# A written-out order of operations replaced by another: warming products first, keys loaded in halves, block means of v transposed once per batch

## The chip, the core and the metric

The kernel runs on one NeuronCore of one Trainium2 chip. The metric is the device time of one execution in microseconds (us). Three runs of the kernel before gave 411.3, 411.57 and 408.1 us.

## The reference

Four batches, 768 positions, 8 heads of 64. Attention of each query over its near keys (less than 16 positions away) and over 24 block summaries, one for each 32 positions: the maximum of the keys, the mean of the values. Its output, 512 wide, goes through a gated layer with a product over positions.

```python
k_sum = k.reshape(B, H, nb, 32, D).max(axis=3)
v_sum = v.reshape(B, H, nb, 32, D).mean(axis=3)
scores_l = scale * q @ k.T            # kept where |i - j| < 16
scores_s = scale * q @ k_sum.T + log(32)
a = softmax(concat(scores_l, scores_s));  x = a @ concat(v, v_sum)
h = maximum(x @ w_in, 0);  u, v = h[..., :512], h[..., 512:]
v_n = (v - mean(v)) / sqrt(var(v) + 1e-6)
v_s = w_spatial @ v_n + b_spatial[:, None]     # over positions
out = (u * v_s) @ w_out
```

## The kernel before

**Attention.** A group is one batch `b`, one third `c` of its queries (256 positions) and one half `g` of its heads: 24 groups. For each there is a block of scores (`s{b}_{c}_{g}`, 32 instructions, line 431), a softmax (`m...`: masked minimum on VectorE at line 444, exponential on ScalarE at line 448, normalisation at line 459 or 461 on ScalarE, VectorE or GpSimd), a transpose of the probabilities (`t...`, lines 480 and 488) and the product with the values (`x...`, line 504). The keys come from HBM as one tile for each batch and pair of heads (`key_load`, `k{b}_{pr}`, 544 KB); `key_prep` (tag `p{b}_{pr}`) takes maxima on VectorE (line 359) and ScalarE copies them behind the keys of each segment (line 369). Of batch 0 the block means of v come from a product (`vsums`, tag `vs`, line 384); of batches 1 to 3 from `vmean` (tag `vm`): one load of `vT`, one sum on VectorE (line 403) and one transpose on TensorE (line 407) for each of the four pairs of heads.

**The gated layer.** Every product is three products of split numbers (a high and a low part, both fp32r, `mm3`, line 538): `pv` (the half of `w_in` for v), `pu` (the half for u), `sp` (over positions), `po` (output). The weights come in 64-bit words and are converted by `split64`, a chain of seven to nine operations on ScalarE, VectorE and GpSimd; for the four pieces `wi1_*` of the v half three products on TensorE (lines 298 to 300) make the low part, which ScalarE then copies out. The first product of `pv0_0` or `pv0_1` waits for all four pieces `wi1_*` and for `x0_0_0` and `x0_0_1` (line 539: the first step carries the needs of all).

**The order.** `Plan` collects operations; each can run on the engines it names. `ORDER` lists them all: two characters of base 64 are the number of an operation, a digit is its engine (0 PE, 1 VectorE, 2 ScalarE, 3 GpSimd, 4 the DMA queue of SyncE). `Plan.order` places them in this order and works out a start for each, with its own constants for engines, lags and transfers. Each engine, and the one queue SP that issues nearly all loads and stores, then executes its operations strictly in the listed order. The starts are used for one more thing: as long as the warming product `warm` (128 x 120, two instructions) has a last use ahead, lines 731 to 733 put one more of them in front of a TensorE operation for each 330 ns of planned idle time. In the table of before the first warming product stands eleventh on TensorE, after `s0_1_0`; its last use follows `t0_1_1`.

The last output tile (`last`, lines 632 to 636) is evicted from PSUM in two halves of 64 partitions, one by ScalarE with a store from ScalarE's queue, one by VectorE with a store from SP.

Of the kernel before, what the change touches and what calls it, by code (L numbers as in the profile page):

```python
# [9 lines left out]
F32 = mybir.dt.float32  # L10
# [27 lines left out]
ONES = QB + (NT - 1) * (P // SBLK)  # L38
# [25 lines left out]
class Plan:  # L64
# [7 lines left out]
    TURN_ROUND, TURN_OVER = 187, 143  # L72
# [4 lines left out]
    def add(self, engs, fn, pri, w=(), r=(), port=False, xfer=0, mode="d", lat=0, tag=None):  # L77
# [7 lines left out]
        op.ready = op.start = op.end = 0  # L85
        after = set()
# [20 lines left out]
    def order(self):  # L107

        free = dict(SP=730, POOL=5500)
# [39 lines left out]
        while pool:  # L149
            op, e = listed[len(made)] if listed else choose()  # L150
            at = max([a.end if a.eng == e else a.done for a in op.after], default=0)
# [29 lines left out]
            for u in op.users:  # L181
                u.need -= 1
                u.ready = max(u.ready, op.end if e == "PE" and "PE" in u.engs else done + (SLACK if "PE" in u.engs and not listed else 0))
                if not u.need:
                    pool.append(u)
# [6 lines left out]
def tile_local_summary_attention_gmlp(ctx: ExitStack, tc: tile.TileContext, qT, kext, vext, vnat, vT, w_in, w_sp, b_rep, w_out, out):  # L192
# [49 lines left out]
    def dma(out_, in_, kb, pri, w=(), r=(), issue=400, rate=RATE, tag=None):  # L242
# [104 lines left out]
    def key_load(b, pr, pri):  # L347
        kt = k_sb[b, pr] = Buf(att, [P, KC], F32, "k", f"k{b}_{pr}")
        dma(lambda: kt.t, kext[b, pr], 544, pri, w=[kt], tag=f"k{b}_{pr}")

    def key_prep(b, pr, pri):
        kt = k_sb[b, pr]
        gm = Buf(small, [P, 52], F32, "gm", f"gm{b}_{pr}")
        plan.tag = f"p{b}_{pr}"

        def emit(e):
            t, g = kt.t, gm.t
            kv = t[:, :NSEG * SEG].rearrange("p (s c) -> p s c", c=SEG)
# [461 lines left out]
def psa_ns(n):  # L820
    return 58 + n * 0.828
# [60 lines left out]
```

## Time and profile before

| | us |
|---|---|
| median of three runs | 411.3 |
| the profiled execution | 409.42 |
| its span, first to last instruction | 407.6 |
| PE (TensorE matmul) busy in it | 388.2 |
| DVE (VectorE) busy | 277.4 |
| ACT (ScalarE) busy | 196.8 |
| POOL (GpSimd) busy | 62.6 |
| mean granted TensorE clock (1 is 2.4 GHz) | 0.989 |

Times in rows are microseconds from the start of the span, durations in microseconds or, where a mean of one instruction is given, in nanoseconds. A line number is that of the kernel before.

### The profile page before, as it was taken

To read this page: it belongs to the slowest core of one execution; us is meant where nothing else is said; L and a number is where in the kernel's file an instruction comes from. 1 tells how busy PE (TensorE), PEld (TensorE's weight loads), DVE (VectorE), ACT (ScalarE), POOL (GpSimd) and SP (SyncE) were. 2 spreads that over 40 slices of the span, in tenths; PEclk is the share of its full clock that TensorE was granted. 3 is DMA by queue.
4 is the path that set the end of the run, shared out by engine and by line. 5 is a ranking of instruction groups with operands and counts; after the bars stand their busy time and mean duration, and the time that the engine had idled before them with its cause. 6 is when DMAs were issued, how large, how long until landed. Compare 5 with 4: busy or idle time off the path is not lost.

```text
span 407.6 us, 9242 instructions
## 1 busy us (share of the span) xinstructions
PE 388.2 (95%) x3496; PEld 323.4 (79%) x3496; DVE 277.4 (68%) x964; ACT 196.8 (48%) x645; POOL 62.6 (15%) x91
## 2 busy tenths in 40 slices
PE   2798989999999999999999999999999999999995
PEld 0367868888988888898888888898888888888884
DVE  3989999999956777875675478776786324744421
ACT  2889987886655276642053356635245212200111
POOL 3036556302220002020000030010000000200000
PEclk9969999999999999999999999999999999999998
DMA  8989899530204754301046242302222001000012
GB/s 282 406 240 285 254 303 317 143 112 2 90 28 166 225 193 143 104 7 61 0 117 197 73 158 66 92 2 67 66 67 90 27 2 53 2 0 0 27 51 77
DMA packets 18684, 46.86 MB, mean 115 GB/s; under 512 B 2512, under 2 KB 3280, under 8 KB 18512
## 3 DMA queue, kind: packets, MB, share of 16 engines
q1 hardware_dynamic: 18560, 46.15, 36.1%
q8 instruction: 27, 0.44, 0.4%
q10 hardware_dynamic: 80, 0.13, 0.1%
q14 instruction: 17, 0.14, 0.1%
HBM read 39.98 MB, written 6.29 MB: 114 GB/s over the span
## 4 chain that ended last, share of the span: by engine, by line
PE 87%; DMA 5%; DVE 3%; ACT 2%; SPq 1%; issue 1%; POOL 1%; DVEq 0%
PE sp L538 24%; PE po L538 15%; PE pu L538 15%; PE pv L538 15%; PE s L431 6%; PE x L504 6%; DMA k<-in_kext_dram 3%; PE t L488 3%; PE t L480 1%; DMA wi<-in_w_in_dram 1%; SPq L243 1%; ACT p L448 1%; DVE gm L359 1%; PE wwi L298 0%; POOL p L461 0%
## 5 line engine op out<-in xcount | busy, mean ns | idle before, releaser
L448 ACT ACTIVATE p<-p,sums 128x120 f32<-128x120 f32 x192 | 73.7, 387 | 6.3 <-DVE sums L444 6.1
L538 PE MATMUL sp<-wsp_h,vnh 128*128 128x512 f32 (+1 forms) x192 | 65.2, 339 | 0.0
L538 PE MATMUL sp<-wsp_l,vnh 128*128 128x512 f32 (+1 forms) x192 | 64.6, 337 | 0.0
L538 PE MATMUL sp<-wsp_h,vnl 128*128 128x512 f32 (+1 forms) x192 | 64.6, 336 | 0.0
L444 DVE CUSTOM_DVE_ANT_0 p<-s,mask 128x120 f32<-128x120 f32 x192 | 42.2, 276 | 12.7 <-PE s L431 12.7
L538 PE MATMUL po<-wo_h,gt 128*128 128x512 f32 x128 | 46.2, 395 | 0.0
L538 PE MATMUL pu<-xh,win_h 128*128 128x512 f32 (+1 forms) x128 | 43.8, 342 | 0.0
L606 DVE TENSOR_TENSOR g<-sp,brep 128x512 f32<-128x512 f32 (+1 forms) x32 | 17.3, 555 | 38.5 <-PE sp L538 38.2
L538 PE MATMUL pu<-xl,win_h 128*128 128x512 f32 (+1 forms) x128 | 43.1, 337 | 0.0
L538 PE MATMUL pu<-xh,win_l 128*128 128x512 f32 (+1 forms) x128 | 43.1, 337 | 0.0
L538 PEld LDWEIGHTS sp<-wsp_h,vnh 128*128 128x128 f32 x192 | 36.4, 190 | 4.5
L538 PEld LDWEIGHTS sp<-wsp_l,vnh 128*128 128x128 f32 x192 | 36.4, 190 | 4.1
L538 PEld LDWEIGHTS sp<-wsp_h,vnl 128*128 128x128 f32 x192 | 36.4, 190 | 3.8
L538 PE MATMUL pv<-win_h,xh 128*128 128x512 f32 x96 | 38.5, 401 | 0.8 <-DVE g L606 0.8
L572 POOL TENSOR_TENSOR mv<-mv,mhalf 128x1 f32<-128x1 f32 x24 | 14.5, 605 | 154.7 <-DVE mv L571 142.7
L538 PE MATMUL po<-wo_l,gt 128*128 128x512 f32 x96 | 37.6, 391 | 0.0
L538 PE MATMUL pv<-win_l,xh 128*128 128x512 f32 x96 | 37.6, 391 | 0.0
L538 PE MATMUL pv<-win_h,xl 128*128 128x512 f32 x96 | 37.4, 390 | 0.0
L448 ACT ACTIVATION_READ_ACCUMULATOR p<-p,sums 128x1 f32 x192 | 36.5, 190 | 0.0
L249 ACT COPY pt<-t 120x512 f32<-120x512 f32 x31 | 17.9, 584 | 28.5 <-PE t L488 25.2
L253 ACT ACTIVATE u<-pu 128x256 f32<-128x256 f32 (+1 forms) x27 | 13.0, 485 | 37.3 <-PE pu L538 37.2
L569 DVE BATCH_NORM_STATS2 mv<-vf 128x6 f32<-128x512 f32 x24 | 16.5, 687 | 19.0 <-ACT vf L253 19.0
(128 smaller groups left out, 766.1 us busy)
## 6 DMA issues: line engine op xcount, KB each, us to landing
k<-in_kext_dram SPq DMA_DIRECT2D x16, 544.0 KB, 7.2
qd<-in_qT_dram SPq DMA_DIRECT2D x24, 256.0 KB, 4.4
ve<-in_vext_dram SPq DMA_DIRECT2D x24, 256.0 KB, 3.9
out_dram<-ob SPq DMA_DIRECT2D x23, 256.0 KB, 2.0
vt<-in_vT_dram SPq DMA_DIRECT2D x12, 384.0 KB, 4.8
wi<-in_w_in_dram SPq DMA_DIRECT2D x6, 512.0 KB, 7.2
ve<-in_vext_dram SPq DMA_DIRECT2D x24, 128.0 KB, 3.6
wo<-in_w_out_dram SPq DMA_DIRECT2D x8, 256.0 KB, 5.4
```

Source lines behind the costliest of these rows:

```text
L243: add(("SP", issue), lambda e: nc.sync.dma_start(out=out_() if callable(out_) else out_, in_=in_() if callable(in_) else in_), pri, w, r, ...
L249: (nc.scalar.copy if e == "ACT" else nc.vector.tensor_copy)(out=out_, in_=in_)
L253: nc.scalar.activation(out=out_, in_=in_, func=AF.Relu)
L431: nc.tensor.matmul(out=ps.t[r * QB:(r + 1) * QB, a, i * KW:(i + 1) * KW], lhsT=qt[hs, r, i], rhs=kts[r].t[hs, g * SEG:g * SEG + KW], start ...
L444: add(("DVE", 203), lambda e, i=i, mi=mi: nc.vector.tensor_tensor_reduce(out=pt.t[:, i, :], in0=ps.t[:, a, i * KW:(i + 1) * KW], in1=mask[ ...
L448: add(("ACT", 380), lambda e, i=i: nc.scalar.activation(out=pt.t[:, i, :], in_=pt.t[:, i, :], func=AF.Exp, scale=-1.0, bias=st.t[:, 0, i:i ...
L488: nc.tensor.transpose(out=ps.t[:KW, r, a * CH + i * QB:a * CH + (i + 1) * QB], in_=pts[a].t[hs, i, :], identity=ident[hs, hs])
L504: nc.tensor.matmul(out=ps.t[a * D:(a + 1) * D, r, n * QB:(n + 1) * QB], lhsT=ve[buf][:, n, o:o + D], rhs=rhs(n, a, r), start=True, stop=True)
L538: nc.tensor.matmul(out=ps.t[:, :n], lhsT=x, rhs=y, start=(j == i == 0), stop=(j == last and i == 2))
L569: add(("DVE", 600), lambda e: nc.vector.bn_stats(out=mv.t[:, 2:], in_=vf.t), pri, w=[mv], r=[vf])
L572: add(("POOL", 560), lambda e: nc.gpsimd.tensor_tensor(out=mv.t[:, 1:2], in0=mv.t[:, 1:2], in1=mhalf, op=ALU.pow), pri, w=[mv])
L606: add(("DVE", dve_ns(n)), lambda e: nc.vector.tensor_add(out=g.t[:, :n], in0=ps.t[:, :n], in1=brep[:, ts]), pri, w=[g], r=[ps, "brep"])
```

## The change

- The first TensorE operation is now `warm`; every other TensorE operation depends on it (`"go"`), so idle time of TensorE in the plan is filled with warming products from the start to the last use of `warm`.
- `ORDER` is another table. The plan's constants differ (SP free at 900 instead of 730 ns, an issue 460 instead of 400 ns, a transfer 2,700 ns and 1 ns for each 410 bytes instead of 2,300 ns and 365 bytes, a lag behind an operation of the same engine).
- The keys of the first two pairs of heads of batch 0 come in two loads each (292 and 251 KB), and `key_prep` reduces each half by itself.
- `vmean` collects the sums of all four pairs of a batch in one 128-column tile, and one transpose serves all four: 3 transposes instead of 12.
- The last tile is evicted in two halves of 256 columns.

Decoded, the two tables begin so (operations of TensorE, then of SP; `wi1_2` stands for the three products of a piece, `dk0_1_1` is the second half of a key tile):

```
before PE  wi1_1 s0_0_0 wi1_2 wi1_0 t0_0_0 s0_0_1 wi1_3 t0_0_0 vs s0_1_0 warm t0_0_1 x0_0_0 t0_0_1 s0_1_1
           x0_0_1 t0_1_0 t0_1_0 s0_2_0 x0_1_0 pv0_1 pv0_1 pv0_0 ...
after  PE  warm s0_0_0 s0_0_1 t0_0_0 s0_1_0 t0_0_0 wi1_2 vs t0_0_1 s0_1_1 x0_0_0 t0_0_1 wi1_0 wi1_1 x0_0_1
           t0_1_0 s0_2_0 (last warm) t0_1_0 wi1_3 x0_1_0 pv0_0 pv0_0 pv0_0 pv0_1 ...
before SP  dwi1_1 dk0_1 dk0_0 dwi1_2 dq0_0_0 dwi1_3 dwi1_0 dwi0_3 dk0_3 dwi0_2 dk0_2 dwi0_3_256 dq0_0_1
           dvn dws4_0 dq0_1_0 dvt1_0 dh0_0_0 dv0_0_0 dws5_512 dq0_1_1 ...
after  SP  dk0_1_1 dk0_1_0 dk0_0_0 dk0_0_1 dwi0_2 dq0_0_0 dk0_3 dwi1_1 dwi0_3_256 dk0_2 dq0_0_1 dws1_0
           dwi1_0 dwi1_2 dvt1_0 dq0_1_0 dwi0_3 dq0_1_1 dvn dwi1_3 dh0_0_0 dws0_512 dv0_0_0 ...
```

From `s1_2_0` (about 124 us) on, the two orders of TensorE differ only in the transposes of `vmean`.

```diff
-    TURN_ROUND, TURN_OVER = 187, 143
+    OWN = dict(PE=0, ACT=140, DVE=120, POOL=90, SP=0)
+    TURN_ROUND, TURN_OVER, TURN_BACK = 187, 143, 120
...
+        if "PE" in op.engs:
+            r = (*r, "go")
...
-        free = dict(SP=730, POOL=5500)
+        free = dict(SP=900, POOL=5500)
...
-            at = max([a.end if a.eng == e else a.done for a in op.after], default=0)
+            at = max([a.end + self.OWN[e] if a.eng == e else a.done for a in op.after], default=0)
...
     def key_load(b, pr, pri):
-        dma(lambda: kt.t, kext[b, pr], 544, pri, w=[kt], tag=f"k{b}_{pr}")
+        for n, (lo, hi) in enumerate(halves(b, pr)):
+            dma(lambda lo=lo, hi=hi: kt.t[:, lo * SEG:min(hi * SEG, KC)], kext[b, pr][:, lo * SEG:min(hi * SEG, KC)], 544 * (hi - lo) // (NSEG + 1), pri, w=[(kt, n)], r=[kt], tag=f"k{b}_{pr}_{n}")
+
+    def halves(b, pr):
+        return ((0, NSEG // 2), (NSEG // 2, NSEG + 1)) if (b, pr // 2) in SPLIT_K else ((0, NSEG + 1),)
...
+    def vmean(b, pri):
+        for pr in range(NPAIR):
+            plan.tag = f"vm{b}_{pr}"
+            vt = Buf(att, [P, S], F32, "vt", f"vt{b}_{pr}")
+            dma(lambda vt=vt: vt.t, vT[b, pr], 384, pri + VT_OFF, w=[vt], tag=f"vt{b}_{pr}")
+            add(("DVE", 863), lambda e, vt=vt, pr=pr: nc.vector.tensor_reduce(
+                out=vs_in[:, b % 2, pr * SBLK:pr * SBLK + NS], in_=vt.t.rearrange("p (n e) -> p n e", e=SBLK),
+                axis=AX.X, op=ALU.add), pri + VM_OFF, w=[f"vs{b % 2}_{pr}"], r=[vt])
+        ps = Buf(ps_m, [P, 512], F32, "m", f"vmp{b}")
+        plan.tag = f"vm{b}"
+        add(("PE", 130), lambda e: nc.tensor.transpose(out=ps.t[:, :P], in_=vs_in[:, b % 2], identity=ident), pri, w=[ps], r=[f"vs{b % 2}_{pr}" for pr in range(NPAIR)])
...
-                nc.scalar.copy(out=ob.t[:D], in_=ps.t[:D])
-                nc.scalar.dma_start(out=out[b, t * P:t * P + D, :], in_=ob.t[:D])
-                nc.vector.tensor_copy(out=oc.t[D:], in_=ps.t[D:])
-                nc.sync.dma_start(out=out[b, t * P + D:(t + 1) * P, :], in_=oc.t[D:])
+                nc.scalar.copy(out=ob.t[:, :TH], in_=ps.t[:, :TH])
+                nc.scalar.dma_start(out=out[b, rows, :TH], in_=ob.t[:, :TH])
+                nc.vector.tensor_copy(out=oc.t[:, :TH], in_=ps.t[:, TH:])
+                nc.sync.dma_start(out=out[b, rows, TH:], in_=oc.t[:, :TH])
...
-    add(("PE", 200), lambda e: nc.tensor.matmul(out=warm.t[:, :KW], lhsT=ident, rhs=ident[:, :KW], start=True, stop=True), -99, w=[warm])
+    add(("PE", 200), lambda e: nc.tensor.matmul(out=warm.t[:, :KW], lhsT=ident, rhs=ident[:, :KW], start=True, stop=True), -99, w=[warm, "go"])
...
-        if b and c == 0:
-            for r in range(2):
-                vmean(b, 2 * g + r, pri, buf)
+        if b and c == 0 and g == 1:
+            vmean(b, pri)
...
+SPLIT_K = ((0, 0),)
-WIRE, RATE, RATE_64, RATE_32 = 2300, 365.0, 330.0, 300.0
+WIRE, RATE, RATE_64, RATE_32 = 2700, 410.0, 200.0, 200.0
```

## Rows read from the trace of the kernel before

**Rows 1.** The stretches of the span: PE, PEld, DVE, ACT and POOL busy in us with their instructions, then the granted clock, the DMA share and GB/s.

```profile
40.38:66.31 25.93, 23.95 (x256) 19.41 (x253) 24.40 (x96) 22.63 (x76) 14.64 (x15) 1.00 0.95 277
66.31:402.92 336.61, 335.82 (x2892) 285.67 (x2890) 220.04 (x739) 144.27 (x472) 32.83 (x42) 1.00 0.26 81
0.00:40.38 40.38, 28.41 (x355) 18.28 (x355) 32.22 (x131) 29.33 (x98) 15.10 (x36) 0.92 0.91 305
```

**Rows 2.** The chain that ended last, in order of time: start, duration, what.

```profile
11.52 1.92 PE s L431 x32
...
28.39 0.98 PE s L431 x32
...
35.01 0.86 PE warm L733 x6
...
39.30 1.15 PE x L504 x32
40.45 3.63 PE pv L538 x15
...
44.95 0.22 PE warm L701 x2
```

**Rows 3.** What TensorE waited for from 40.4 us to the end: us in total, times, longest.

```profile
PE t L480 <- ACT pt L249: 1.7, 1, 1.7
PE pv L538 <- DVE g L606: 0.8, 1, 0.8
```

**Rows 4.** The timeline of TensorE in the first 66 us: start, duration, engine, line, operation, out<-in.

```profile
7.43 2.05 PE L298 MATMUL wwi<-wi,ident 128*128 128x512 f32 x2 [7.43 <-DVE wi L283]
...
16.54 1.13 PE L298 MATMUL wwi<-wi,ident 128*128 128x512 f32 x2 [0.28 <-DVE wi L283]
```

**Rows 5.** The granted clock by half microseconds: stretch, PE busy, PEclk, DMA share, GB/s.

```profile
14.00:14.50 0.50, 0.50 (x3) 1.00 0.95 264
...
20.00:20.50 0.50, 0.00 (x0) 0.50 0.89 373
...
26.00:26.50 0.50, 0.50 (x3) 0.50 0.94 184
26.50:27.00 0.50, 0.50 (x8) 0.98 0.94 193
```

**Rows 6.** The timeline of all engines in the first 35 us: the matrix for the warming products, the first exponential.

```profile
1.30 0.29 POOL masks.py:199 TENSOR_SCALAR_AFFINE_SELECT ident<-ident 128x128 f32<-128x128 f32 x1
...
13.90 0.40 ACT L448 ACTIVATE p<-p,sums 128x120 f32<-128x120 f32 x1 [0.58 <-DVE sums L444]
```

**Rows 7.** DMA bytes in the first 7.5 us: as in the first group, by stretches of 2.5 us.

```profile
0.00:2.50 2.50, 0.00 (x0) 0.00 (x0) 0.00 (x0) 1.28 (x1) 1.88 (x11) 1.00 0.20 56
2.50:5.00 2.50, 0.00 (x0) 0.00 (x0) 0.00 (x0) 0.00 (x0) 2.08 (x14) 1.00 0.95 258
5.00:7.50 2.50, 0.07 (x1) 0.10 (x1) 1.30 (x3) 1.05 (x3) 0.03 (x1) 1.00 1.04 418
```

**Rows 8.** ScalarE's instructions by line and form: count, busy us and mean ns of one, then idle time before them.

```profile
L448 ACT ACTIVATE p<-p,sums 128x120 f32<-128x120 f32 x192 | 73.7, 387 | 6.3 <-DVE sums L444 6.1
...
L249 ACT COPY pt<-t 120x512 f32<-120x512 f32 x31 | 17.9, 584 | 28.5 <-PE t L488 25.2 <-PE t L480 2.3 <-DVE pt L249 0.9
L459 ACT ACTIVATE p<-p,sums 128x120 f32<-128x120 f32 x44 | 13.6, 386 | 8.9 <-DVE sums L454 8.9
...
L253 ACT ACTIVATE u<-pu 128x256 f32<-128x256 f32 x14 | 5.4, 383 | 13.0 <-PE pu L538 13.0
...
L281 ACT ACTIVATE wi<-wi 128x512 f32<-128x512 f32 x6 | 4.0, 673 | 3.4 <-DMA wi<-in_w_in_dram 3.4
...
L249 ACT CAST wsp_h<-ws 128x512 fp32r<-128x512 f32 x3 | 1.9, 618 | 0.0
```

**Rows 9.** Two stretches between the first scores and `pv0`: columns as in the first group.

```profile
13.57:38.40 24.83, 21.32 (x266) 14.02 (x270) 23.40 (x112) 21.86 (x80) 10.66 (x12) 0.86 0.93 294
13.90:39.25 25.35, 21.70 (x286) 14.24 (x284) 23.89 (x111) 22.71 (x82) 10.66 (x12) 0.87 0.93 295
```

**Rows 10.** The timeline of SP's queue in the first 30 us.

```profile
11.26 0.33 SPq L243 DMA_DIRECT2D vn<-in_vnat_dram  x1
...
23.58 0.33 SPq L243 DMA_DIRECT2D qd<-in_qT_dram  x1
```

**Rows 11.** The transposes of `vmean`, one pair of them in the chain that ended last.

```profile
164.94 0.35 PE vmp L407 x2
```

**Rows 12.** The DMA issues of the page: count, KB each, median us from issue to landing.

```profile
qd<-in_qT_dram SPq DMA_DIRECT2D x24, 256.0 KB, 4.4
```

**Rows 13.** The end of the timeline.

```profile
402.95 0.58 ACT L633 COPY ob<-po 64x512 f32<-64x512 f32 x1 [2.13 <-PE po L538]
...
403.56 0.69 DVE L635 COPY oc<-po 64x512 f32<-64x512 f32 x1 [5.71 <-ACT ob L633]
404.29 0.52 SPq L636 DMA_DIRECT2D out_dram<-oc  x1
```

**Rows 14.** VectorE's instructions by line and form, as for ScalarE above.

```profile
L359 DVE TENSOR_REDUCE gm<-k 128x48 f32<-128x768 f32 x16 | 15.1, 946 | 7.5 <-DMA k<-in_kext_dram 7.5
...
L283 DVE SCALAR_TENSOR_TENSOR wi<-wi 128x512 int32<-128x512 int32 x6 | 4.0, 689 | 0.1
...
L255 DVE TENSOR_SCALAR u<-pu 128x256 f32<-128x256 f32 x2 | 0.8, 414 | 0.0
```

More of the change, by code (lines that the diff above doesn't have):

```diff
@@ L37 @@
 NT = S // P
-ONES = QB + (NT - 1) * (P // SBLK)
+ONES = (NT - 1) * (P // SBLK)
 TH = 256
@@ L182, in order @@
                 u.need -= 1
-                u.ready = max(u.ready, op.end if e == "PE" and "PE" in u.engs else done + (SLACK if "PE" in u.engs and not listed else 0))
+                u.ready = max(u.ready, op.end + self.OWN[e] if e in u.engs and len(u.engs) == 1 else done + (SLACK if "PE" in u.engs else 0))
                 if not u.need:
@@ L384, in mm @@
                     nc.tensor.matmul(
-                        out=ps.t[pr * SBLK:pr * SBLK + NS, :P], lhsT=vs_in[:, o:o + NS], rhs=vn.t[:, t, pr * P:(pr + 1) * P], start=t == 0, stop=t == NT - 1)
-        add(("PE", VS_NS), mm, pri + VM_OFF, w=[ps], r=["ones", vn], mode="v")
+                        out=ps.t[pr * SBLK:pr * SBLK + NS, :P], lhsT=vs_one[:, o:o + NS], rhs=vn.t[:, t, pr * P:(pr + 1) * P], start=t == 0, stop=t == NT - 1)
+        add(("PE", VS_NS), mm, pri + VM_OFF, w=[ps], r=[vn], mode="v")
         for pr in range(NPAIR):
@@ L396, in vspread @@
             nc.vector.tensor_scalar_mul(out=out_, in0=in_, scalar1=1.0 / SBLK)
-    def vmean(b, pr, pri, buf):
-        plan.tag = f"vm{b}_{pr}"
-        vt = Buf(att, [P, S], F32, "vt", f"vt{b}_{pr}")
-        dma(lambda: vt.t, vT[b, pr], 384, pri + VT_OFF, w=[vt], tag=f"vt{b}_{pr}")
-        vs = vs_in[:, pr * SEG:(pr + 1) * SEG]
-        add(("DVE", 863), lambda e: nc.vector.tensor_reduce(
-            out=vs[:, QB:], in_=vt.t.rearrange("p (n e) -> p n e", e=SBLK),
-            axis=AX.X, op=ALU.add), pri + VM_OFF, w=[f"vs{pr}", "ones"], r=[vt])
-        ps = Buf(ps_m, [P, 512], F32, "m", f"vmp{b}_{pr}")
-        add(("PE", 85), lambda e: nc.tensor.transpose(out=ps.t[:SEG, :P], in_=vs, identity=ident), pri, w=[ps, f"ves{buf}_{pr % 2}"], r=[f"vs{pr}"])
-        add(dict(ACT=psa_ns(512), DVE=dve_ns(512)), lambda e: vspread(e, ps.t[QB:SEG, :P], buf, pr), pri, w=[f"ves{buf}_{pr % 2}"], r=[ps])
+    def vmean(b, pri):
[9 more added lines that the diff above has]
+        add(("PE", 130), lambda e: nc.tensor.transpose(out=ps.t[:, :P], in_=vs_in[:, b % 2], identity=ident), pri, w=[ps], r=[f"vs{b % 2}_{pr}" for pr in range(NPAIR)])
+        for pr in range(NPAIR):
+            plan.tag = f"ve{b}_{pr}"
+            add(dict(ACT=psa_ns(512), DVE=dve_ns(512)), lambda e, pr=pr: vspread(e, ps.t[pr * SBLK:pr * SBLK + NS, :P], pr // 2, pr), pri, w=[f"ves{pr // 2}_{pr % 2}"], r=[ps])
     def q_load(b, c, g, buf, pri):
@@ L433, in mm @@
                         rhs=kts[r].t[hs, g * SEG:g * SEG + KW], start=True, stop=True)
-        return S_NS, mm, [ps], [*kts, f"q{buf}"], "s", lambda pri: [softmax((b, c, pg, a), ps, pri) for a in range(2)]
+        return S_NS, mm, [ps], [*kts, *[(kt, n) for kt in kts for n in range(2)], f"q{buf}"], "s", lambda pri: [softmax((b, c, pg, a), ps, pri) for a in range(2)]
     def softmax(u, ps, pri):
```

136 lines of the change are left out of this document (71 added, 65 removed).

## The prediction

> **What bounds the kernel now.** I read the stretches of the span first, then the chain that ended last, then the waits of each engine. From 66 us to the end of the products at 402.9 TensorE is busy 335.8 of 336.6 us, and between 40.4 and 66 us 23.9 of 25.9 [rows 1]; there only shorter TensorE work or fewer of its gaps can help. Before 40.4 us it is busy 28.4 of 40.4, part of that at half clock. `pv`, the first long run of products, begins at 40.4 [rows 2]. So the end is: start of `pv`, plus the products behind it, plus their gaps (1.7 and 0.8 us are the large ones [rows 3]), plus the last tile. The change moves the first term by its order, the second by the transposes, the fourth by the halves. The sum is made against the profiled execution, 409.42 us (span 407.6 and 1.8 around it). That lies 1.9 below the median of the runs and 0.7 below the mean of the three runs and itself, 410.1.
>
> **Warming products.** The same pair of fp32 products took 2.05 us at 7.4 and 1.13 at 16.5 us [rows 4], one block of scores 1.92 us at 11.5 and 0.98 at 28.4 [rows 2]. So the first products run at 1.2 GHz, although the column of the granted clock reads 1.00 at 14 us, before any event; later it does show the fall (0.50 at 20.0) and the rise at 26.5, after TensorE had worked back to back from 20.6 [rows 5].
>
> How many warming products stand ahead of `s0_0_0`? By the plan's constants its keys, the `w_in` piece and q land at 6.77, 7.41 and 8.05 us, ScalarE's copy of the second key tile ends at 8.09 and counts 0.14 later: start 8.23. The first product ends at 0.20 in the plan, and 8,030/330 gives 24 more: 25. A product is two instructions; six took 0.86 us in the chain [rows 2], so I take 0.29 us for a product at 2.4 GHz and, by the ratios 1.8 and 1.96 of the pairs above, 0.55 at 1.2. Their matrix is there at 1.6 us [rows 6]. If all ran cold: 25 x 0.55 from 1.7, to 15.4; all warm: to 9.0. The stretch that is nearest, an engine busy back to back from a cold start, took 5.9 us to the rise (20.6 to 26.5 [rows 5]); by that 11 products are cold, 14 not: 1.7 + 5.9 + 4.1 = 11.7. The scores then take 0.98 and end at **12.7**. In the kernel before they ended at 13.4.
>
> Their data would be there sooner. In the kernel before 140 KB had arrived by 2.5 us, 785 by 5.0 and 1,830 by 7.5 [rows 7]. The first 512 KB landed at 5.4, when 960 KB had come in all (others share the queues); with the same surplus of 450 KB the four key halves land at 4.9, 5.5, 6.1 and 6.8 us, and q (1,600 KB in) at 8.1. VectorE's reduction of the last half and ScalarE's copy end near 8.4. So what the halves bring, 3 us, is spent behind 25 warming products, and VectorE and ScalarE, which execute in order, wait for the scores from about 9 to 12.8 us.
>
> **The work between first scores and `pv`.** The needs of the first `pv` are the same: four `wi1` pieces, `x0_0_0`, `x0_0_1`; the same TensorE blocks stand ahead of it. What differs is how much of ScalarE's and VectorE's lists stands between the first scores and its last need. Counted in the two tables and priced by the rows of each form (an exponential with its read 0.385, from start to start): ScalarE before, from the first exponential to the `t0_1_0` copies: 51 operations, 24.4 us. After, to the copy `wi1_3`: 62 operations, 32.4 us. The 8.0 more: two normalisations of four instructions (3.1), three first scalings of 512 columns (2.0), a cast, a `ws` cast of 512 and one of 256 (1.6), a `pt` and an `xh` copy (1.2), an exponential (0.4), a `negid` (0.3), less a `vs` copy (0.6) [rows 8]. Three of those scalings and their chains were done ahead of the first scores; now keys stand there. VectorE: 77 operations, 26.3 us before; 84, 31.3 us after (the chains of the `wi1` pieces, one more `vm` sum).
>
> ScalarE did its 24.4 us in a stretch of 25.35, busy 22.7 (operations overlap their neighbours); VectorE its 26.3 in 24.8, busy 23.4 [rows 9]. By the same ratios the new lists are 30.2 us of ScalarE and 27.9 of VectorE. ScalarE's first exponential comes 0.46 behind the scores, as before (13.44 to 13.90): 13.2. Without any idle time it reaches the gate at 43.4, with the 2.6 us that it idled before at 46.0. VectorE: 12.8 + 27.9 = 40.7, then three products (about 1.9) and a copy (0.6): 43.2 or, with its 1.4 idle, 44.6. I take the middle of ScalarE's two: `pv` begins at 44.7, **+4.3**. If the products were all warm the scores would end at 10.0 and `pv` begin at 40.7 to 43.3.
>
> **What comes back.** The 1.7 us gap at 55.4 is a wait for ScalarE's copy of `t0_2_0` [rows 3]. From the gate to that copy ScalarE has as much to do as before (19.0 and 18.7 us), but TensorE now has 20 steps of `pv` and `pu` ahead of it instead of 16, 0.69 each: 2.8 us more cover. The gap closes: -1.7. Two warming instructions behind `pv` (0.22 [rows 2]) move ahead of it. Together **-2.0**, bounds -2.8 and +1.5 (a wait as long elsewhere).
>
> **Transposes.** Twelve, 0.175 each by the pair [rows 11], are 2.1 us on a full TensorE. Three remain; 128 columns instead of 88, bounds 0.175 and 0.3: **-1.6**. All four pairs must be summed first; VectorE has 220 busy of 337 us there [rows 1], and the 12 sums and loads stay.
>
> **Last tile.** ScalarE's copy of 64 x 512 ran 0.58, and VectorE's of 0.69 began only when it had ended, though the partitions differ [rows 13]. A copy of 128 x 256 takes 0.38 on ScalarE and 0.41 on VectorE [rows 8, 14]. One behind the other they end 0.48 earlier; side by side 0.86. Rows of 1 KB in place of 2 KB may cost the stores up to 0.8. I take **-0.5**.
>
> The Trainium skill (PSUM — Partial Sum Buffer, section PSUM bank collisions) says that two engines must not touch the same bank and 32-partition quadrant at once, and that different quadrants may be read together. By that, halves of 64 partitions could have been copied side by side and halves of columns can't. The trace disagrees on the first (the wait ends with ScalarE's copy, 403.56), so the form that the page allows was not faster here, and serial copies stay my estimate.
>
> **Free or nearly so.** Two more reductions (at most 0.16 each, VectorE idles there) and two more loads (0.33 on SP ahead of the first landing). Behind 124 us the tables hold the same order but for the transposes.
>
> Sum: 409.42 + 4.3 - 2.0 - 1.6 - 0.5 = 409.6; on the mean of the four executions, **410.3 us**: about the same as before.
>
> **Rivals.** *Faster: TensorE warms early and ScalarE never idles.* If the clock comes up at once, `s0_0_0` ends at 10.0 and `pv` begins at 40.7, +0.3: 409.42 + 0.3 - 4.1 = 405.6, on the mean 406.3. It is beyond 1% when `pv` begins before 40.4. For it: TensorE never falls back to half clock between 20 and 26.5, where the chain of before ran through its scores and transposes. Against: VectorE and ScalarE were 94 and 90% busy in that stretch [rows 9], so TensorE's slow stretch cost them little. The Trainium skill (TensorE: Matmul & The Clock Gate, section What's actually happening) says that the throttled state is the default and activity releases it; the slow first rows agree, and by it warming products do release the clock but can't start warm.
>
> *Slower: SP's queue stands still behind a q load.* In the table q of `s0_1_1` comes ahead of `vn` (1,536 KB), `wi1_3` and the v tiles; it must wait until `s0_0_1` has read its buffer. In the kernel before `vn` went out at 11.3, that q at 23.6 [rows 10], when the scores had ended. Now `s0_0_1` needs the fourth key tile prepared: VectorE 5.5 and ScalarE 4.5 us of list behind 12.8, so scores from about 18.5 to 19.5. Then 2,304 KB to the end of `wi1_3` at some 400 KB/us, 5.8 us, and about 4.4 for landing [rows 12]: 29.7. ScalarE, with 17.7 us of its list (16.5 by the ratio) ahead of `wi1_3`, reaches it at 13.2 + 16.5 = 29.7. It decides from there on: each us that the scores are later goes one to one into ScalarE's list, into `pv` and the end. 4 us of it give 414.3. For it: the estimate stands on the edge. Against: waits of SP are free as long as ScalarE is late too.
>
> *No effect at the start.* If the longer lists only replace idle time, `pv` stays near 41.5 and the time is 407, within 1%.
>
> **The numbers.** Within 1% (some 4 us, about what a measurement of this kernel tells from no change): 0.58, the forecast with the third rival. Faster by more: 0.17, the first rival with a little more. Slower by more: 0.25, the second, or ScalarE idling more than before. The range, 405.5 to 416.0, reaches to the first rival's end with no gap left and to a queue that costs 5 us.
>
> **What would show it.** Right: 25 warming products ahead of the first scores, these ending near 12.7 us; VectorE idle from about 9; `pv` at 43 to 46.5; no gap of 1.7 us at `t0_2_0`; one `vmp` instruction for each batch; VectorE's last copy behind ScalarE's. Wrong: scores ending by 10.5 or after 14.5, `pv` before 41 us; ScalarE waiting for `wi1_3` or `vs`; a second fall of the clock; new gaps on TensorE behind 66 us, where I see no cause for any.

## The result and the profile after

| | before | after |
|---|---|---|
| time, median of 22 runs, us | 408.46 (407.35 to 411.57) | 410.77 (410.02 to 412.65) |
| ratio | | 1.0055, 95% interval 1.0041 to 1.0069 |
| profiled execution: span, us | 407.6 | 409.0 |
| first scores begin / end, us | 11.5 / 13.4 | 10.4 / 11.4 |
| `pv` begins, us | 40.4 | 43.9 |
| last product ends to end of span, us | 4.65 | 3.46 |

The changed kernel is 0.55% slower: 2.3 us by the medians, 1.4 us between the two profiled executions. The difference of these two is in the kernel before: its profiled execution (409.42 us) lay 0.96 above the median that 22 runs gave, while that of the changed kernel (410.78) is its median. One execution of e15 and one of e16 below took 2183.44 and 985.75 us; they are in the medians of the table there and not in its ratios.

Busy time by stretches of the changed kernel, columns as in [rows 1]: up to `pv`, to 66 us, to the last product, and the last 10.9 us ahead of `pv`.

```profile
0.00:43.87 43.87, 34.48 (x455) 28.31 (x455) 34.52 (x136) 32.15 (x105) 14.81 (x36) 1.00 0.94 298
43.87:66.31 22.44, 21.17 (x214) 17.10 (x211) 22.14 (x83) 19.88 (x70) 10.02 (x10) 1.00 0.93 278
66.31:405.50 339.19, 337.87 (x2923) 287.00 (x2921) 223.81 (x749) 146.68 (x478) 33.47 (x44) 1.00 0.27 81
...
32.95:43.87 10.92, 10.36 (x155) 7.46 (x155) 10.61 (x40) 10.82 (x35) 4.36 (x5) 1.00 0.92 255
```

The clock column no longer falls [rows 5]. `pv` comes 3.5 us later than in [rows 2], and in the last line three engines are full at once: TensorE 95%, VectorE 97%, ScalarE 99%. The start of the timeline of TensorE, then of ScalarE:

```profile
2.23 7.33 PE L748 MATMUL warm<-ident 128*128 128x120 f32 x48
10.36 1.05 PE L447 MATMUL s<-k,qd 64*64 64x120 f32 x32 [0.81 <-ACT k L382]
```

```profile
5.59 0.43 ACT L382 COPY k<-gm 128x288 f32<-128x288 f32 x1
9.55 0.43 ACT L286 ACTIVATE wf<-wi 128x256 f32<-128x256 f32 x1 [3.54 <-DMA wi<-in_w_in_dram]
9.89 0.42 ACT L382 COPY k<-gm 128x288 f32<-128x288 f32 x1
```

The 25 warming products end at 9.56. TensorE then waits for ScalarE's copy of the second key tile, and that copy stands behind the scaling of a `w_in` piece whose load landed 7.0 us after its issue at 2.58.

What TensorE waited for from 38 us to the end (answers to [rows 3]: us in total, times, longest):

```profile
PE t L496 <- ACT pt L254: 1.0, 1, 1.0
PE pu L554 <- ACT vf L258: 1.0, 1, 1.0
PE pv L554 <- ACT ve L407: 0.4, 1, 0.4
PE t L496 <- DVE vf L589: 0.2, 1, 0.2
PE s L447 <- DVE sums L460: 0.2, 1, 0.2
```

Behind `pv` (the last line lies ahead of it) that is some 2.6 us of gaps, where the kernel before had 2.8. The 1.7 us gap at `t0_2_0` is gone, as is the one of 0.8. In their place stand one at `t0_1_1` (49.06), one at 82.05 and one of 0.4 at 264.99. The last two on TensorE's timeline:

```profile
82.05 0.39 PE L554 MATMUL pu<-xh,win_h 128*128 128x256 f32 x1 [0.97 <-ACT vf L258]
...
264.99 0.50 PE L554 MATMUL pv<-win_h,xh 128*128 128x512 f32 x1 [0.35 <-ACT ve L407]
```

From the start of `pv` to the last product the kernel before took 362.57 us, the changed one 361.67.

A transpose of the block means: first the kernel before, then the changed one, both on TensorE's timeline.

```profile
164.88 0.42 PE L407 MATMUL vmp<-ident,vs_in 128*88 128x128 f32 x2
165.05 0.48 PE L538 MATMUL pv<-win_h,xh 128*128 128x512 f32 x1
```

```profile
85.39 0.27 PE L421 MATMUL vmp<-ident,vs_in 128*128 128x128 f32 x1
85.59 0.64 PE L447 MATMUL s<-k,qd 64*64 64x120 f32 x16
...
262.25 0.27 PE L421 MATMUL vmp<-ident,vs_in 128*128 128x128 f32 x1
262.27 0.47 PE L554 MATMUL po<-wo_h,gt 128*128 128x512 f32 x1
```

From start to next start such a pair took 0.17 us, one of the new form 0.02 to 0.20. The end of the timeline (answers to [rows 13]):

```profile
405.54 0.37 ACT L649 COPY ob<-po 128x256 f32<-128x256 f32 x1 [2.13 <-PE po L554]
405.94 0.37 ACTq L650 DMA_DIRECT2D out_dram<-ob  x1
405.94 0.42 DVE L651 COPY oc<-po 128x256 f32<-128x256 f32 x1 [5.50 <-ACT ob L649]
406.40 0.33 SPq L652 DMA_DIRECT2D out_dram<-oc  x1
```

The copies still follow each other, as expected. They and the issue of the last store are shorter (0.33 for 0.52), and the store landed in 1.7 us where the one of 2 KB rows took 2.3. In all 3.46 us in place of 4.65. The balance of the two executions: +3.5 (start of `pv`) - 0.9 (products and gaps behind it) - 1.2 (last tile) = +1.4. The kernel e1 below differs from the kernel before in the last tile alone. Its trace (TensorE, then ScalarE, whose last copy waits for the last product) has `pv` at 40.09 and the end of the last product 361.88 us behind that, without the gap of 0.8:

```profile
40.09 0.50 PE L538 MATMUL pv<-win_h,xh 128*128 128x512 f32 x1
...
401.97 0.37 ACT L633 COPY ob<-po 128x256 f32<-128x256 f32 x1 [2.13 <-PE po L538]
```

Against that trace the start of `pv` costs 3.8, the stretch behind it gives 0.2 and the last tile 1.2: +2.4, which is what the medians show. So most of the 0.9 above lies in the one execution of the kernel before that was profiled.

### The profile page after: what moved, and what is told of

Its sections match the earlier page's. It is cut to its first block, busy times and chain, and to the rows that moved or that the text cites. A ratio compares the mean times of both kernels' runs of the same rounds, so it can differ in the third digit from the quotient of the medians.

```text
span 409.0 us, 9425 instructions
## 1 busy us (share of the span) xinstructions
PE 393.5 (96%) x3585; PEld 332.4 (81%) x3585; DVE 280.9 (69%) x965; ACT 199.1 (49%) x652; POOL 58.3 (14%) x89
## 4 chain that ended last, share of the span: by engine, by line
PE 79%; DVE 12%; DMA 4%; ACT 3%; issue 1%; SPq 1%; DVEq 0%; ACTq 0%
PE sp L554 25%; PE po L554 16%; PE pu L554 14%; PE pv L554 12%; PE x L520 5%; PE s L447 4%; PE t L504 3%; DMA vt<-in_vT_dram 2%; DMA k<-in_kext_dram 2%; DVE p L460 1%; DVE vs_in L416 1%; DVE wi L288 1%; DVE gm L369 1%; ACT ve L407 1%; DVE vf L589 1%
## 5 line engine op out<-in xcount | busy, mean ns | idle before, releaser
L464 ACT ACTIVATE p<-p,sums 128x120 f32<-128x120 f32 x192 | 73.8, 388 | 10.7 <-DVE sums L460 10.6
L460 DVE CUSTOM_DVE_ANT_0 p<-s,mask 128x120 f32<-128x120 f32 x192 | 43.3, 276 | 12.2 <-PE s L447 12.2
L588 POOL TENSOR_TENSOR mv<-mv,mhalf 128x1 f32<-128x1 f32 x24 | 13.6, 568 | 159.8 <-DVE mv L587 141.9
L447 PE MATMUL s<-k,qd 64*64 64x120 f32 x768 | 25.2, 269 | 4.6 <-ACT k L382 2.5
```

The costliest lines, as they stand in the source:

```text
L447: nc.tensor.matmul(out=ps.t[r * QB:(r + 1) * QB, a, i * KW:(i + 1) * KW], lhsT=qt[hs, r, i], rhs=kts[r].t[hs, g * SEG:g * SEG + KW], start ...
L460: add(("DVE", 203), lambda e, i=i, mi=mi: nc.vector.tensor_tensor_reduce(out=pt.t[:, i, :], in0=ps.t[:, a, i * KW:(i + 1) * KW], in1=mask[ ...
L464: add(("ACT", 380), lambda e, i=i: nc.scalar.activation(out=pt.t[:, i, :], in_=pt.t[:, i, :], func=AF.Exp, scale=-1.0, bias=st.t[:, 0, i:i ...
L588: add(("POOL", 560), lambda e: nc.gpsimd.tensor_tensor(out=mv.t[:, 1:2], in0=mv.t[:, 1:2], in1=mhalf, op=ALU.pow), pri, w=[mv])
```

## The experiments

All ratios are to the kernel before, run on the same chip. `pv` is its start in the profiled execution.

| run | what it is | median, us | ratio, 95% interval | `pv` |
|---|---|---|---|---|
| e1 | before + halves by columns | 407.24 | 0.9974, 0.9958 to 0.9991 | 40.1 |
| e2 | before + one transpose per batch | 408.29 | 1.0020, 0.9991 to 1.0050 | 40.1 |
| e3 | before + warming first | 407.89 | 0.9986, 0.9969 to 1.0003 | 39.7 |
| e5 | these three, old order | 408.16 | 1.0002, 0.9984 to 1.0020 | 39.3 |
| e13 | halves and warming, old order | 407.25 | 0.9964, 0.9943 to 0.9986 | 39.5 |
| e4 | after without filling | 412.86 | 1.0103, 1.0079 to 1.0127 | 45.3 |
| e8 | after, first `w_in` piece later | 412.38 | 1.0102, 1.0085 to 1.0119 | 45.5 |
| e9 | old order, head of the new | 414.74 | 1.0153, 1.0132 to 1.0174 | 47.3 |
| e10 | new order, head of the old | 417.24 | 1.0230, 1.0207 to 1.0253 | 48.7 |
| e6 | after, ScalarE work deferred | 416.01 | 1.0182, 1.0159 to 1.0205 | 43.9 |
| e7 | after, VectorE work deferred | 422.78 | 1.0354, 1.0332 to 1.0376 | 42.7 |
| e11 | after, ScalarE +2.7 us | 411.93 | 1.0088, 1.0068 to 1.0107 | 44.9 |
| e12 | after, VectorE +2.4 us | 412.94 | 1.0113, 1.0093 to 1.0133 | 45.9 |
| e14 | after, 2.0 us from VectorE to ScalarE | 412.91 | 1.0104, 1.0074 to 1.0134 | 45.6 |
| e15 | after, VectorE -1.7 us | 410.76 | 1.0049, 1.0028 to 1.0070 | 43.4 |
| e16 | after, ScalarE -2.5 us (to GpSimd) | 411.62 | 1.0069, 1.0046 to 1.0093 | 45.3 |
| e17 | e15 and e16 | 410.67 | 1.0049, 1.0022 to 1.0076 | 44.3 |
| e18 | after, one TensorE piece earlier | 410.51 | 1.0041, 1.0020 to 1.0062 | 42.9 |

**The parts alone.** e1 has the tail's four new lines in the kernel before; e2 the new `vmean`, its transpose where the last of the four stood; e3 the dependency `"go"` and the first warming product at the head of the table:

```diff
+        if "PE" in op.engs:
+            r = (*r, "go")
```

> The kernel before with one part of the change: its last tile is copied and stored by column halves (128 x 256) in place of row halves (64 x 512). Theory T1 (the 1.2 us that the changed kernel has less between the last product and the end of the span, 3.46 for 4.65, is all due to the halves): the same 1.2 us less here, ratio 0.997. Rival (the shorter copies alone, 0.5 us, as the prediction had it, the rest being chance of the stores' landing): 0.5 less, ratio 0.999.

> The kernel before with one part of the change: the block means of v are transposed once per batch, where the last of the four old transposes stood, and ScalarE spreads the four pairs right behind. T1 (the transposes on a full TensorE were worth less than the 1.6 us of the prediction; the changed kernel's stretch from pv to the last product is 0.9 shorter, gaps included): 0.5 to 0.9 us less, ratio 0.998. Rival (the prediction's 1.6 is right, and the changed kernel loses a part of it in new gaps): 1.6 less, ratio 0.996.

> The kernel before with one part of the change: TensorE begins with the warming products, as many as its plan puts ahead of the first scores (about 30), order of everything else as before. T1 (TensorE's half clock ahead of pv costs little, as VectorE and ScalarE are over 90% busy there and set the start of pv): the first scores take 1.0 in place of 1.9 us, pv begins 0 to 1 us earlier, at 39.4 to 40.4, the time falls by 0 to 1 us, ratio 0.998 to 1.000. Rival (the cold scores and transposes from 11.5 to 26.5 us hold VectorE and ScalarE up): pv begins at 37 to 38.5, the time falls by 2 to 3.5 us, ratio 0.992 to 0.995.

The halves gained 1.0 us, about as much as the two traces had shown. Warming first came out 0.6 lower by the ratio, in an interval that just holds no change; `pv` came 0.7 us earlier. Both are in T1's range and far from the rival's. The transposes gained nothing that the times show. e2's fastest execution (407.08) lay level with the fastest of before (407.27), and 5 of its 12 lay between 409.5 and 412.8; what was longer in these no profile here shows, as the profiled one is the fastest.

e5 is all three with the old order, e13 only the first and the third:

> All parts of the change but the order: the table of the kernel before, with the warming products first, one transpose per batch and the last tile by column halves. T1 (the new order alone makes the changed kernel slower, by what pv starts later): pv begins at 39.5 to 40.1, the gains of the three parts add up to 1.3 to 2.3 us, ratio 0.9945 to 0.997; the order itself then costs 3.5 to 4.5 us. Rival (the parts were worth something only with the new order, or cost something without it, as the single run of the transposes at 1.002 could mean): ratio 0.998 to 1.002.

> The kernel before with the two parts that were faster alone: warming products first and the last tile by column halves; order and transposes of v as before. If these two add up: 0.9974 x 0.9986 = 0.996, pv at 39.5 to 40, 1.6 us less than before. If the one transpose per batch is worth its 0.8 us in every execution, the run of all parts with the old order (1.0002) would have to lie below this one; if it costs, this one is the fastest.

The gains didn't add up in e5: 1.0002 lies above T1's range and inside the rival's. Its profiled execution has `pv` at 39.3 and a span of 404.5, but its runs spread from 406.2 to 410.5. The mean granted clock goes with that in part: the five executions at 0.996 or less took 407.8 to 410.5, the seven at 0.998 or more 406.2 to 409.1; what else made them longer stays open. e13, without the transposes, is 0.36% faster than before and has the lowest ratio here. The order itself, the changed kernel against e5, costs 0.5% or about 2.2 us by the medians and 3.8 by the fastest executions (410.02 and 406.23); in the profiles `pv` comes 4.6 us later.

**The start.** e4 sets the filling to zero, e8 moves the first `w_in` piece behind the copy of the second key tile:

```diff
-WARM, WARM_TO = 1 / 330, 1
+WARM, WARM_TO = 0.0, 1
```

> The changed kernel without the filling: one warming product at the start and one behind pv, none of the 24 between. T1 (the warming products don't hold the first scores, ScalarE's copy of the second key tile does, and the order's longer lists set the start of pv): the first scores begin at 10.4 as in the changed kernel and end about 1 us later, at 12.3, at half clock; pv begins 0 to 2 us later than 43.9, the time is 0 to 2 us longer, ratio to the kernel before 1.005 to 1.010. Rival (the 25 products ahead of the first scores delay them, as the prediction said): scores begin at 8.5 to 9, pv 1 to 3 us earlier, ratio 0.998 to 1.003.

> The changed kernel with the operations on the first w_in piece (two on ScalarE, three on VectorE) moved behind the copy of the second key tile, so that ScalarE doesn't wait for that piece's load ahead of the first scores; the lists up to pv hold the same work. T1 (ScalarE's wait for the piece released the first scores at 10.4, the warming products had ended at 9.6): scores begin at 9.0 to 9.7 behind the warming products; pv 0 to 0.8 us earlier, time 0 to 0.8 us shorter than the changed kernel. Rival (the prediction's: the warming products release the scores): they begin at 10.2 or later, pv unchanged.

In e4 the scores begin at 10.6, so the warming products didn't hold them; they take 1.88 us, and the time is 2.1 us longer than with the filling. The new order needs the warming products, the old one hardly (0.6, not clear of zero). In e8 neither theory met: ScalarE's wait was gone, the warming products ended at 9.98, and the next thing was late.

```profile
10.54 1.05 PE L447 MATMUL s<-k,qd 64*64 64x120 f32 x32 [0.55 <-DMA qd<-in_qT_dram]
```

In the changed kernel three needs of the first scores lie within a microsecond: the warming products (9.56), q (issued at 3.05, landed 7.1 us later: 10.15) and the key copy (10.31). In e8 q landed 7.4 us after its issue and came last. The second scores came 2.0 us later than in the changed kernel and `pv` 1.6; a part of that may be the clock, which in this trace fell to half from 20 to 24 us.

**The order, crossed.** e9 and e10 join the two tables at ScalarE's first exponential:

> The changed kernel's code with two tables joined: the new order through the first exponential on ScalarE (key halves, one w_in piece, first scores), everything behind it in the old order. T1 as it stands now (with the keys first ScalarE and VectorE have 2.4 and 2.9 us less work behind them at the first exponential than in the kernel before, and that comes back ahead of pv): pv begins 1.5 to 3 us later than in the run of all parts with the old order, 39.3, so at 40.8 to 42.3, ratio 1.003 to 1.007. Rival (the later part of the new order costs, the early scores are a gain of about 1 us): pv at 38.3 to 39.5, ratio 0.997 to 1.000.

> The reverse: the old order through the first exponential (two w_in pieces ahead of and among the keys, which are loaded in halves), everything behind it in the new order. T1: pv begins 1.5 to 2.5 us earlier than in the changed kernel, at 41.4 to 42.4, ratio 1.000 to 1.003. Rival (the later part of the new order costs): pv at 43.5 to 45, ratio 1.005 to 1.009. If both this run and the one with the new head lie between, each part has its share.

Both are much slower than either order, so neither theory is told. At the seam the loads no longer come in the order in which the engines want them: ScalarE of e9 and VectorE of e10 stand still (both timelines):

```profile
20.05 0.66 ACT L286 ACTIVATE wi<-wi 128x512 f32<-128x512 f32 x1 [6.44 <-DMA wi<-in_w_in_dram]
```

```profile
25.80 0.43 DVE L254 CAST wsp_h<-ws 128x512 fp32r<-128x512 f32 x1 [4.21 <-DMA ws<-in_w_sp_dram]
```

**Work deferred.** e6 and e7 move operations in the table from ahead of the first `pv` to behind it (e7: three loads too), with what follows on them:

```diff
 e6, ScalarE, ahead of pv0_0:
-ws0_512.0  ws4_0.0  ws3_512.0  wi0_2_256.0  wi0_1_0.0
 e7, VectorE and SP, ahead of pv0_0:
-ws1_0.0  vm1_0.0  vm1_1.0  wi0_2_256.1  and the loads of vt1_1, vt1_2, vt1_3
```

> The changed kernel with five ScalarE conversions that the first pv doesn't need (three ws casts, the first scalings of wi0_2_256 and wi0_1_0, 2.2 us in the changed kernel's timeline) moved from ahead of pv to behind it, with what follows on them. T1 (ScalarE's list between the first scores and pv sets when pv begins): pv begins 1.7 to 2.2 us earlier than 43.9, at 41.7 to 42.2; the time falls by 1 to 2.2 us against the changed kernel, as far as no gap behind pv grows, ratio to the kernel before 1.000 to 1.003. Rival (VectorE's list, 95% busy in that stretch, or the chain through both sets it): pv begins at 43.2 or later, time within 0.7 us of the changed kernel.

> The changed kernel with VectorE work that the first pv doesn't need (a ws cast, two sums of v for the second batch and an operation of wi0_2_256, 2.4 us in the changed kernel's timeline) moved from ahead of pv to behind it, with the three v loads of that batch. T1 (ScalarE alone sets pv, VectorE has slack): pv at 43.2 to 43.9, time within 0.7 us of the changed kernel, ratio to the kernel before 1.004 to 1.006. Rival (VectorE's list sets pv): pv at 41.5 to 42.3, the time 1.5 to 2.4 us shorter. Both engines in turn: pv about 1 us earlier.

e6 left `pv` where it was, e7 brought it 1.2 us earlier, and both lost more behind it. In e7 the deferred sums share the buffers of the v tiles, so each load waits for the sum before; VectorE stands in order behind the loads (6.4 and 2.9 us), and TensorE waits 12.1 us. In e6 ScalarE waits 1.6 us for VectorE at 48.6. VectorE had itself waited 1.55 us for a deferred scaling of ScalarE (to 44.41), and a small operation of it at 48.60 took 1.22 us, where the same line takes 0.16 in e7 (56.61). TensorE then waits 3.9 us, and its clock falls. TensorE's timeline of e6, then its granted clock by stretches:

```profile
51.97 1.11 PE L496 MATMUL t<-ident,p 128*120 128x128 f32 x4 [3.92 <-ACT pt L254]
53.01 1.88 PE L447 MATMUL s<-k,qd 64*64 64x120 f32 x32
54.81 1.97 PE L520 MATMUL x<-pt,ve 120*64 120x64 f32 x32
```

```profile
50.00:54.00 4.00, 2.03 (x24) 1.70 (x28) 4.00 (x11) 3.00 (x10) 1.23 (x2) 0.58 0.67 179
54.00:58.00 4.00, 4.00 (x56) 3.40 (x49) 3.87 (x6) 2.20 (x6) 2.61 (x3) 0.57 0.74 187
58.00:62.00 4.00, 4.00 (x20) 3.27 (x19) 4.00 (x16) 3.17 (x14) 1.28 (x2) 1.00 0.86 264
```

Scores of 1.88 for 1.05 and an output block of 1.97 for 1.15 us: the gap cost some 2 us more than itself. So these two runs say what deferring costs, little of what sets `pv`.

**Lists made longer.** No load, buffer or order changes; instructions are done twice:

```diff
-copy(e, hi, fv())                                  (e11: six w_in casts on ScalarE)
+[copy(e, hi, fv()) for _ in range(2)]
-nc.vector.scalar_tensor_tensor(out=low(), ...)     (e12: the last operation of each wi1 piece)
+[nc.vector.scalar_tensor_tensor(out=low(), ...) for _ in range(2)]
```

> The changed kernel with six of ScalarE's casts of w_in pieces ahead of pv done twice (2.7 us more on ScalarE by the timeline, no load or buffer touched). If ScalarE's list sets pv: pv 2 to 2.7 us later, 45.9 to 46.6, time 2 to 2.7 longer, ratio 1.010 to 1.013. If VectorE's does and ScalarE waits for it: pv less than 0.8 later, ratio 1.005 to 1.0075.

> The changed kernel with the last VectorE operation of the four wi1 pieces done twice (2.4 to 2.8 us more on VectorE by the timeline, no load or buffer touched). If VectorE's list sets pv: pv 2 to 2.8 us later, 45.9 to 46.7, ratio 1.010 to 1.0125. If ScalarE's does: pv less than 0.8 later, ratio 1.005 to 1.0075. If the two wait for each other in turn, both this run and the one with ScalarE's casts doubled come out at more than half their added work.

ScalarE's 2.7 us moved `pv` by 1.1, VectorE's 2.4 by 2.0; the medians rose by 1.2 and 2.2. Each of the two hits `pv`, ScalarE's less: its waits for VectorE between 12 and 44 us, 2.3 us in the changed kernel, fell to 0.8 and took up a part. (In e11 TensorE also ran at half clock from 33 to 37 us, its output block 1.70 for 1.15 us; how much of the 1.1 that is stays open.) That looked like VectorE (T3), so e14 gave three operations of VectorE to ScalarE, and e15 left out 23 of the 24 block sums of v for two pairs of heads:

```diff
 e14
-wi1_2_0.7 VectorE   vs0.0 VectorE   vs3.0 VectorE
+wi1_2_0.7 ScalarE   vs0.0 ScalarE   vs3.0 ScalarE
 e15, the sums of pairs 0 and 1 of batch 1
-in_=vt.t.rearrange("p (n e) -> p n e", e=SBLK)
+in_=vt.t.rearrange("p (n e) -> p n e", e=SBLK)[:, :1]
```

> The changed kernel with three operations ahead of pv (two spreads of block means, the last copy of wi1_2; 2.0 us) moved from VectorE to ScalarE, where they take about 1.8 us; no load or buffer touched. Theory T3 (VectorE's list sets pv, with about 0.85 us for each us added, ScalarE's with 0.4): pv 0.7 to 1.3 us earlier, at 42.6 to 43.2, time 0.5 to 1.3 shorter than the changed kernel, ratio 1.0025 to 1.0045. T1 (ScalarE's list sets pv, as the prediction had it): pv 1 to 1.8 us later, ratio 1.008 to 1.010.

> The changed kernel with 1.6 to 1.7 us of VectorE's work ahead of pv left out: the sums of v for two pairs of the second batch cover one block of 32 rows in place of all 24 blocks (their loads stay). T3 (VectorE's list sets pv): pv 1.2 to 1.7 us earlier, at 42.2 to 42.7, ratio to the kernel before 1.0015 to 1.003. T1 (ScalarE's list sets pv): pv within 0.5 of 43.9, ratio 1.004 to 1.006.

T3 fell: `pv` came 1.7 us later in e14, 0.5 earlier in e15, both on T1's side; by the ratio e15 doesn't differ from the changed kernel (1.0049 and 1.0055). In e14 the first output block waits 1.9 us for a spread on ScalarE, where it waited 1.2 for one on VectorE. So ScalarE was relieved, alone and with VectorE:

```diff
 e16, and with e15's sums e17
-m0_0_0.10 ScalarE   m0_1_0.21 ScalarE
+m0_0_0.10 GpSimd    m0_1_0.21 GpSimd
```

> The changed kernel with two normalisations of scores (each four instructions, 1.24 us on ScalarE) given to GpSimd, where the order of the kernel before has them and where they take 1.0 us each; GpSimd is busy 10 of 32 us there. No load or buffer touched. Theory T4 (ScalarE's and VectorE's lists wait for each other and are nearly equally long, so pv follows the later of the two): ScalarE's 2.5 us come back only until VectorE's list is the later one, pv 0.5 to 1.5 us earlier, at 42.4 to 43.4, ratio 1.002 to 1.0045. T1 (ScalarE's list alone): pv 2 to 2.5 us earlier, at 41.4 to 41.9, ratio 0.999 to 1.001. If GpSimd's start of them is later than ScalarE's was, pv no earlier.

> The same and, as in the run with sums left out, 1.6 to 1.7 us less of VectorE's work ahead of pv (sums of v of two pairs of the second batch over one block of 32 rows in place of 24). T4: with both lists shorter pv comes 1.7 to 2.3 us earlier than in the changed kernel, at 41.6 to 42.2, more than the two cuts gave alone taken together, ratio 0.999 to 1.0015. T1: no earlier than with the normalisations moved alone.

Neither brought `pv` forward (45.3, 44.3): both misses for T1 and T4. In e16's trace TensorE ran at half clock from 22 to 26 us (its scores at 22.36 took 1.64 us for 1.05, granted clock 0.50), so its 45.3 holds more than the change; e17's ran at full clock. The plan sees more idle time on TensorE there and fills it: between the second output block and `pv` 8 warming instructions in place of 2, some 0.6 us. The busy times of e17 from its first output block to `pv`:

```profile
32.88:44.28 11.40, 11.19 (x160) 8.21 (x160) 11.04 (x44) 10.15 (x33) 5.82 (x6) 1.00 0.89 268
```

ScalarE has slack there (10.15 of 11.40), and TensorE, with the filling, is full (11.19). TensorE, the third engine, was relieved last: one of the three pieces that the new order puts behind the first output block, where the old one has none, moved ahead. So that no new filling takes its place, e18 also ends the filling at 30 us of the plan.

```diff
-... t0_0_0.0 ... t0_0_1.0  wi1_0_0.6  wi1_1_0.6  x0_0_1.0        (TensorE)
+... wi1_1_0.6  t0_0_0.0 ... t0_0_1.0  wi1_0_0.6  x0_0_1.0
-wi1_1_0.7 ahead of pv                                           (ScalarE)
+wi1_1_0.7 behind wi1_2_0.4
-            if warm.made is not None and op.start < warm.ops[-1].start:
+            if warm.made is not None and op.start < 30000:
```

> The changed kernel with TensorE's products for the w_in piece wi1_1 (three lines of the timeline, 1.33 us) moved from behind the first output block of attention, where TensorE is busy 10.4 of the 10.9 us to pv, to ahead of the first transposes at 24.9, where TensorE waits or warms for 1.7 us, and ScalarE's copy of their result with them; no filling products behind 33 us. Theory T5 (TensorE's own list sets pv: the new order puts three such pieces behind that block, the old one had all four ahead of it): pv 1.0 to 1.3 us earlier, at 42.6 to 42.9, ratio 1.002 to 1.0035. T6 (in those 10.9 us TensorE, ScalarE and VectorE are all full, 95, 99 and 97% busy, and wait for each other, so that relief of one gives little): pv within 0.5 us of 43.9, ratio 1.004 to 1.0065.

`pv` began at 42.9, between the two. But all 0.95 us of it were gained ahead of the first output block, which began at 32.00 for 32.95, and 0.8 of them ahead of the moved piece itself: the third scores began at 21.45 for 22.23, the piece at 22.43. From the first output block to `pv` it took 10.92 us, as in the changed kernel: where the piece stood, TensorE now waits for ScalarE. TensorE's timeline of e18, then the busy times:

```profile
34.66 0.40 PE L305 MATMUL wwi<-win_l,negid 128*128 128x512 f32 x1
36.83 1.19 PE L520 MATMUL x<-pt,ve 120*64 120x64 f32 x32 [1.77 <-ACT p L464]
```

```profile
32.00:42.92 10.92, 9.06 (x150) 6.74 (x150) 10.61 (x40) 10.82 (x36) 4.34 (x5) 1.00 0.91 256
```

TensorE has slack now (9.06), ScalarE (10.82 of 10.92) and VectorE (10.61) have as little as in the changed kernel. That speaks for T6: added work on VectorE goes into `pv` nearly in full and on ScalarE by two fifths, and relief of one engine ends at the next.

How far does one trace carry this? The changed kernel, e11, e12 and e14 to e18 have the same list up to the first scores, and these begin anywhere from 9.89 (e16) to 10.71 (e14); e8, e11, e15 and e16 have some 4 us at half clock ahead of `pv`. So a move of `pv` by less than about 0.8 us says little by itself. By the ratios e11, e12 and e14 (1.0088 to 1.0113) are slower than the changed kernel (1.0055), while the four that relieve an engine (1.0041 to 1.0069) can't be told from it. It isn't shown that relief of all three together would bring `pv` to the 39.3 of the old order; that wasn't tried, and neither was the new order of the loads by itself.

## Why the prediction was right or wrong

**The forecast** of about no change (+0.2 us on the executions' mean) stands against +0.55%. The value of 410.3 is near the 410.77 by luck, because the base was high: the mean of the four executions was 410.1, the median of 22 runs is 408.46. On the profiled executions +0.2 stands against +1.4: the start of `pv` and the last tile came out 1.5 us better than forecast, the gaps and transposes behind `pv` 2.7 worse (-0.9 for -3.6).

**The start of `pv`: right.** +4.3 forecast, +3.5 measured, 43.87 inside the range of 43.4 to 46.0 that the lists gave. From the first exponential (12.12) ScalarE was busy 29.07 of 31.75 us and VectorE 30.25, where they had 23.84 and 25.02 of 26.48 in the kernel before: 5.2 more each, for 8.0 and 5.0 counted. Two sources can be read off. Up to the first exponential ScalarE had done 3.08 us of work, before 5.49; VectorE 4.27, before 7.20; this comes back later. The rest, 2.8 and 2.3 us, is work that the old order did behind `pv`. That "the same TensorE blocks stand ahead of it" was right as a count and missed their place: three pieces of products, 4 us, now stand behind the first output block, on a TensorE that is 95% full.

**The first scores: right in direction, wrong in reason.** 11.4, not 12.7. The warming products end at 9.56 instead of 11.7, as a product of two instructions takes less than the price taken from the chain: from start to start an instruction takes 0.21 us up to 6.0 us and 0.11 behind it, so a product 0.43 and 0.22 us, not 0.55 and 0.29. The clock rose near 6.0, 1.6 us earlier than the estimate; in the traces of e3, e5, e8 and e12 the same products quicken between 6.1 and 7.4. Behind that the scores waited for ScalarE's copy, and in e8 for q.

**What comes back: the step that failed.** -2.0 forecast, and that the gap of 1.7 us closes. It closed, but the sum of the gaps is 2.6 for 2.8: the bound "a wait as long elsewhere" was what happened. Behind `pv` ScalarE was still late with the copies for `t0_1_1`, ahead of the one looked at, and new gaps came at 82 and 265 us, where the prediction saw no cause for any. At 82.05 TensorE waits for ScalarE's `vf`, which stands behind casts that wait for VectorE. This gap is the new order's and no chance: it stands in every trace with the new order behind the start but that of e4, and in none with the old one there (before, e1, e2, e3, e5, e9, e13). The old gap of 0.8, in turn, stands in no trace but that of the kernel before.

**Transposes: mis-sized.** Not 1.6 but at most some 0.7 us: by the starts a pair costs 0.17, not the 0.35 that its piece of the chain shows, which runs on to the end of the last product, beyond the start of the next. Twelve are 0.9 us so, three 0.3. The times show none of it (e2, e5), and neither do the traces of e1 and e2: from `pv` to the last product TensorE takes, without its gaps, 359.5 us with twelve and 359.6 with three.

**Last tile: mis-sized.** -0.5 forecast, -1.2 in the traces, -1.0 by e1. The rows of 1 KB cost the stores nothing; the store landed in 1.7 for 2.3 us. The Trainium skill (PSUM — Partial Sum Buffer, section PSUM bank collisions) says that two engines must not touch the same bank and quadrant at once; the copies of 128 partitions fit that, the second starting 0.40 behind the first (405.94, 405.54). But the prediction read too much into the serial copies of row halves when it called them a disagreement with that page. In both forms the trace shows VectorE waiting for ScalarE's copy, an order that the program keeps; what the chip would do without that wait no run here shows.

**The rivals.** The clock was up early, as the faster one said, but ScalarE idled 2.7 us, so it didn't come about. SP's queue did stand still, with q of `s0_1_1` issued at 18.21 and the piece behind it landing at 29.05, but ScalarE came for it at 30.61 and didn't wait: the edge that the slower rival named, by 1.6 us.

## What to carry to other kernels

An order that starts the first result earlier isn't faster if the engines that prepare the rest then have less done: sum what each engine does ahead of the gate that decides, not when the first result comes. Where three in-order engines are full up to a gate, relieving one of them gives little and adding to one may cost in full; and moved work drags its buffers and loads along. Price an operation on a full engine from start to next start, and treat a gap that closes as one that may open elsewhere until the next waits behind it are counted.

## What the hardware showed beyond that

The granted clock reads 1.00 all through the start, though the warming instructions start 0.21 us apart up to 6 us and 0.11 behind it, a factor of 1.9; e4's scores of 1.88 us at 10.6, behind one warming product, show the half clock (1.2 GHz) too. After a gap of 3.9 us in e6 the column did show the fall (0.58). The Trainium skill (TensorE: Matmul & The Clock Gate, section What's actually happening) has the throttled state as the default; e4 agrees.

Loads issued close together landed after very different times: the two 256 KB loads issued at 2.58 and 3.05 took 7.0 and 7.1 us, the four key halves issued ahead of them 2.8 to 5.2. Between 4.5 and 7.5 us the queues moved 172 GB/s, in the kernel before 398; why they were slower no run here shows.
